# One transfer for the queries of a unit, a strided rounding to order them, and a reordered start, in an attention kernel with routed experts

## The chip, the cores and the metric

The kernel runs on one core of a Trainium2 chip. The metric is device time in microseconds (us), from the first to the last work of one execution; the time of a kernel is the median of its runs. The profile is one further execution, recorded by the hardware profiler.

## What is computed

Sliding-window attention with a linear distance bias, then a mixture of experts on its output. The reference, cut to what matters:

```python
# q, k, v: (8 batches, 8 heads, 576 positions, 64)
scores = scale * np.matmul(q, k.transpose(0, 1, 3, 2))
rel = pos[:, None] - pos[None, :]
mask = (rel >= 0) & (rel < 128)
scores = np.where(mask, scores + slopes[:, None, None] * -np.abs(rel), -1e9)
attn = softmax(scores)
x = np.matmul(attn, v).transpose(0, 2, 1, 3).reshape(4608, 512)

y_dense = np.maximum(x @ w1_dense, 0.0) @ w2_dense
expert_idx = np.argmax(x @ w_gate, axis=1)          # 8 experts
for e in range(8):                                   # the token's own expert only
    mask = expert_idx == e
    y_moe[mask] = gate_w[mask, None] * (np.maximum(x[mask] @ w1[e], 0.0) @ w2[e])
return y_dense + y_moe
```

## The kernel before

**Tiling.** Attention is cut into 16 units, `u` from 0 to 15: a batch and four of its eight heads. Each unit has three steps, `pr` 0, 1 and 2, over its five blocks of 128 keys (two, two and one). So there are 48 steps, numbered `n`, in one loop that issues work for several steps at once: scores of step `n`, the attend matmuls of step `n-1`, the normalization of step `n-2`, the transposes of the result (`flip`) of step `n-3`. Each batch, that is, each pair of units, also has a gate (which expert each token goes to), a dense layer in six items spread over the following steps, a scatter of its rows by expert to `xs_dram` and of its dense results to `ys_dram`. After the loop 43 blocks of 128 rows go through the experts (`block`).

**How queries and keys come in.** `load_k` (L125) brings the keys of a unit, 128 partitions by 1152 numbers (18 positions of 64), in one transfer in which each partition's 4608 bytes are one run in memory. `load_q` (L134) brings the queries in five transfers, one for each block of 128 positions, in which a partition gets 4 positions (1024 bytes; 2 positions, 512 bytes, in the last). On VectorE, `turn` (L159, instruction L162) transposes 32 by 32 pieces of either; its results are `ks` and `qs`. `round_qk` (L165) then rounds to the matmul's type on ScalarE: for keys L172 writes with a stride of 18 numbers, which puts the positions in their natural order (`kT`); for queries L169 copies straight through (`qT`), so that the queries within a block stay in another order. The bias mask, built from the iotas of L200 to L217, and the table of token numbers `tok_c` (L294 to L313) follow that order.

**Buffers.** There is one `kraw`, one `qraw`, one `qs` and one `qT` buffer; `kT` has two and the values `vf` three. A load of the next queries can thus start only when `turn` has read the last.

**What sets the order.** PE (TensorE), ACT (ScalarE) and DVE (VectorE) run in the order in which the code is written (`manual_schedule`, L1004). SP, the queue that issues most loads, runs in written order within the loop of 48 steps (L1021 to L1024); ahead of it and behind it, and on POOL (GpSimd), a scheduler orders. In step `pr` 0 of unit `u` stand `turn(u+1, "k")` and `load_k(u+2)`, in step 1 the rounding of the keys, `turn(u+1, "q")` and `load_q(u+2)`, in step 2 `load_v(u+2)`, the rounding of the queries and `prep_v(u+1)` (L182, which splits the values; result `vl`). On DVE L447 (`plo`) makes the low part of the probabilities `p` that ACT has exponentiated (L428), and L496 and L497 normalize (`recip`, `xf`).

**The start.** The queries of unit 0 are issued by ACT (three transfers) and SP (two). L376 is a one-column copy on POOL from the last queries into the values' buffer, which holds one load of the values back until the queries have come. `more_constants` (L279) sets up tables for the gate on DVE, between the transposes of unit 0's keys and queries. `mask_rest` (L275) makes the mask of heads 4 to 7 on ACT.

Of the kernel before, what the change touches and what calls it, by code (L numbers as in the profile page):

```python
# [23 lines left out]
def kernel(  # L24
# [99 lines left out]

    def load_k(u):  # L125
        b, hq = divmod(u, HQ)
        t = ld.tile([P, R, 2, 32], F32, name="kraw", tag="kraw")
        nc.sync.dma_start(
            out=t.rearrange("p r c d -> p (r c d)"),
            in_=k[b, 4 * hq : 4 * hq + 4].rearrange("h (p r) d -> (h p) (r d)", r=R),  # L130
        )
        raw[("k", u)] = t

    def load_q(u, eng):  # L134
        b, hq = divmod(u, HQ)
        hs = slice(4 * hq, 4 * hq + 4)
        t = ld.tile([P, R, 2, 32], F32, name="qraw", tag="qraw", bufs=1)
        for i in range(NT):
            n = 4 if i < NT - 1 else 2
            (eng[i] if isinstance(eng, tuple) else eng).dma_start(  # L140
                out=t[:, 4 * i : 4 * i + n, :, :].rearrange("p r c d -> p (r c d)"),
                in_=q[b, hs, i * P : i * P + 32 * n, :].rearrange(
                    "h (p r) d -> h p (r d)", r=n
                ),
            )
        raw[("q", u)] = t
# [18 lines left out]
    def round_qk(u, nm):  # L165
        s = tmp.pop((nm, u))
        if nm == "q":
            d = qtp.tile([P, 2, S], F32R, name="qT", tag="qT", bufs=1)
            nc.scalar.copy(out=d, in_=s)  # L169
        else:  # L170
            d = kTs[u % 2]
            nc.scalar.copy(  # L172
                out=d[:, :, 0:S].rearrange("p c (x r) -> p c r x", r=R),
                in_=s.rearrange("p c (r x) -> p c r x", r=R),
            )
        qkT[(nm, u)] = d

    def prep_v(u):
# [7 lines left out]

    load_k(0)
    load_q(0, (nc.scalar, nc.sync, nc.scalar, nc.sync, nc.scalar))


# [9 lines left out]
    nc.gpsimd.iota(  # L200
        d_i[:, 0:PW], pattern=[[P, 2], [1, 4], [4, 32]], base=0, channel_multiplier=-1
    )
    nc.gpsimd.iota(
        d_i[:, PW : PW + P], pattern=[[1, 4], [4, 32]], base=0, channel_multiplier=-1
    )
    nc.gpsimd.iota(
        d_i[:, PW + P : PW + P + TAIL],
        pattern=[[1, 2], [2, 32]],
        base=P,
        channel_multiplier=-1,  # L210
    )
    nc.gpsimd.iota(
        d_i[:, PW + P + TAIL : 2 * PW],
        pattern=[[1, 2], [2, 32]],
        base=0,
        channel_multiplier=-1,
    )  # L217
# [61 lines left out]
    def more_constants():  # L279
# [5 lines left out]
        for h in range(2):  # L285
# [8 lines left out]
        nc.vector.tensor_single_scalar(  # L294
            out=m_div, in_=pidx_i, scalar=5, op=ALU.logical_shift_right
        )
        nc.vector.tensor_single_scalar(
            out=m_mod, in_=pidx_i, scalar=31, op=ALU.bitwise_and
        )
        nc.vector.tensor_copy(out=m_divf, in_=m_div)  # L300
        nc.vector.tensor_copy(out=m_modf, in_=m_mod)
        for i in range(NT):
            nc.vector.scalar_tensor_tensor(
                out=tok_c[:, i : i + 1],
                in0=m_modf,
                scalar=4.0 if i < NT - 1 else 2.0,
                in1=m_divf,
                op0=ALU.mult,
                op1=ALU.add,
            )  # L310
            nc.vector.tensor_scalar_add(
                out=tok_c[:, i : i + 1], in0=tok_c[:, i : i + 1], scalar1=float(i * P)
            )  # L313
# [15 lines left out]
    m_div = consts.tile([P, 1], I32, name="m_div")  # L329
    m_mod = consts.tile([P, 1], I32, name="m_mod")  # L330
# [821 lines left out]
```

## Time and profile before

| | |
|---|---|
| time, median of 3 runs | 415.88 us (413.17 to 416.45) |
| the profiled execution's own time | 411.29 us |
| its span, first to last instruction | 409.6 us |
| PE busy | 339.0 us (83%) |
| DVE busy | 269.8 us (66%) |
| ACT busy | 261.6 us (64%) |
| POOL busy | 192.9 us (47%) |
| granted TensorE clock, mean | 0.953 of 2.4 GHz |

How to read the rows of the trace: an engine runs its instructions in order, each for the time shown; behind a row, in brackets, stands how long its engine sat idle before it and what released it. PE is TensorE's matmuls, PEld its weight loads. SPq and ACTq rows are the issuing of transfers, not the transfers. A span is not the sum of busy times: the five engines overlap, and what counts is who waits for whom.

### The profile page before, as it was taken

Reading aid. Unit: us, or ns where it says so; the run is one execution under the profiler, and the core shown is the slowest. Engines: PE = TensorE matmul, PEld = TensorE weight load, DVE = VectorE, ACT = ScalarE, POOL = GpSimd, SP = SyncE. Lnnn points to the kernel's source line nnn. Section 1 sums busy time; section 2 is a strip of 40 time slices with the busy share of each in tenths; the row PEclk is TensorE's granted clock in tenths of the full one; section 3 lists DMA queues with packets and bytes.
Section 4 is the critical chain, followed back from the end, with each engine's and each line's share of the span. In section 5 each row is a group of like instructions: output and inputs, shape, how many; then the busy total and the mean of one; then the engine's idle time right before and its main releaser. Section 6 shows DMA issues by size and latency. Waiting matters only on the chain.

```text
span 409.6 us, 12253 instructions
## 1 busy us (share of the span) xinstructions
PE 339.0 (83%) x4659; PEld 215.2 (53%) x4659; DVE 269.8 (66%) x525; ACT 261.6 (64%) x431; POOL 192.9 (47%) x245
## 2 busy tenths in 40 slices
PE   3458887979869998968997996978799799999990
PEld 0245666646555665645664764654455455555540
DVE  6668889787867986957897889752346344444440
ACT  6448847857856986984797786644356445555550
POOL 4012331654765447564566576353457434434431
PEclk9999959989978999997999998999999999999996
DMA  4565678859798779788696965429959999888730
GB/s 146 144 159 142 148 172 193 195 173 238 165 235 180 202 204 218 212 188 225 197 226 195 235 179 116 99 70 338 310 172 323 303 311 324 244 264 234 250 117 1
DMA packets 84986, 82.40 MB, mean 201 GB/s; under 512 B 43583, under 2 KB 71615, under 8 KB 84928
## 3 DMA queue, kind: packets, MB, share of 16 engines
q1 hardware_dynamic: 66852, 48.17, 41.2%
q0 software_dynamic: 17680, 33.12, 31.3%
q8 instruction: 38, 0.62, 0.6%
q10 hardware_dynamic: 396, 0.33, 0.3%
q14 instruction: 20, 0.16, 0.1%
HBM read 64.20 MB, written 28.66 MB: 227 GB/s over the span
## 4 chain that ended last, share of the span: by engine, by line
PE 30%; DMA 19%; DVE 18%; issue 13%; POOL 9%; SPq 6%; ACT 2%; POOLq 1%; ACTq 0%; DVEq 0%
DMA qraw<-in_q_dram 16%; POOL out_dram L973 6%; DVE plo L447 6%; PE yp L704 6%; PE ax L481 6%; SPq L140 5%; DVE qs L162 4%; PE hpm L937 3%; PE y L964 3%; PE hp L689 3%; DVE xf L497 2%; PE lg L566 2%; DMA xr<-xs_dram 2%; DMA xs_dram<-xrow,slot 2%; PE sq L417 1%
## 5 line engine op out<-in xcount | busy, mean ns | idle before, releaser
L481 PE MATMUL ax<-vf,p 128*128 128x65 bf16 (+1 forms) x576 | 66.6, 205 | 28.8 <-DVE xf L497 26.4
L447 DVE TENSOR_TENSOR plo<-p 128x1024 bf16<-128x1024 f32 (+1 forms) x96 | 85.2, 928 | 8.0 <-ACT p L428 7.9
L481 PEld LDWEIGHTS <-p 128*128 128x128 bf16 (+1 forms) x1152 | 62.9, 107 | 41.3 <-DVE xf L497 34.9
L428 ACT ACTIVATE p<-sq 128x1024 f32<-128x1024 f32 (+1 forms) x96 | 69.8, 784 | 4.8 <-PE sq L417 4.6
L973 POOL DMA_INDIRECT out_dram<-yo,xr x43 | 42.4, 986 | 64.5 <-DVE yo L972 54.1
L503 POOL CAST xrow<-xf 128x512 bf16<-128x512 f32 (+1 forms) x48 | 33.2, 700 | 71.5 <-DVE xf L497 66.7
L481 PE MATMUL ax<-vf,plo 128*128 128x65 bf16 (+1 forms) x576 | 66.1, 202 | 0.5 <-DVE plo L447 0.5
L481 PE MATMUL ax<-vl,p 128*128 128x64 bf16 (+1 forms) x576 | 66.2, 201 | 0.0
L481 PEld LDWEIGHTS <-plo 128*128 128x128 bf16 (+1 forms) x576 | 58.7, 106 | 0.7 <-DVE plo L447 0.7
L713 POOL DMA_INDIRECT ys_dram<-yt,slot x40 | 45.7, 1142 | 26.7 <-ACT yt L712 17.9
L643 POOL DMA_INDIRECT xs_dram<-xrow,slot x40 | 46.2, 1154 | 14.6 <-issue 10.2
L922 DVE COPY xTm<-xps 128x512 bf16<-128x512 bf16 x43 | 18.3, 424 | 50.1 <-PE xps L916 46.9
L696 ACT ACTIVATE hTd<-hp 128x256 bf16<-128x256 f32 (+1 forms) x64 | 26.4, 419 | 35.5 <-PE hp L689 34.6
L937 PE MATMUL hpm<-w_all,xTm 128*128 x172 | 44.0, 377 | 5.1 <-DVE yo L972 2.1
L704 PE MATMUL yp<-w_all,hTd 128*128 128x512 bf16 (+1 forms) x160 | 40.6, 381 | 6.7 <-DVE ltsb L559 5.0
L964 PE MATMUL y<-w_all,hTm 128*128 x172 | 44.1, 379 | 0.8 <-ACT hTm L956 0.8
L945 ACT ACTIVATE hr<-hpm,xr 128x512 bf16<-128x512 f32 x43 | 29.6, 687 | 22.5 <-PE hpm L937 19.3
L972 DVE TENSOR_TENSOR yo<-y,yr 128x512 f32<-128x512 f32 x43 | 29.7, 691 | 20.7 <-PE y L964 20.1
L689 PE MATMUL hp<-xTb,w_all 128*128 128x256 bf16 (+1 forms) x256 | 42.4, 296 | 0.6 <-ACT xTb L531 0.3
L956 ACT COPY hTm<-hps 128x512 bf16<-128x512 bf16 x43 | 25.2, 585 | 23.2 <-PE hps L952 23.2
L531 ACT COPY xT<-tp 128x512 f32<-128x512 f32 (+1 forms) x48 | 23.9, 498 | 23.3 <-PE tp L524 23.2
L417 PE MATMUL sq<-qT,kT 32*128 32x256 f32 (+2 forms) x640 | 32.0, 310 | 7.0 <-ACT qT L169 7.0
(146 smaller groups left out, 559.7 us busy)
## 6 DMA issues: line engine op xcount, KB each, us to landing
yr<-ys_dram SPq DMA_DIRECT2D x43, 256.0 KB
kraw<-in_k_dram SPq DMA_DIRECT2D x16, 576.0 KB
vf<-in_v_dram SPq DMA_DIRECT2D x64, 128.0 KB
w_all<-in_moe_w_dram POOLq DMA_DIRECT2D x16, 512.0 KB
qraw<-in_q_dram SPq DMA_DIRECT2D x62, 128.0 KB
xr<-xs_dram SPq DMA_DIRECT2D x43, 130.0 KB
ys_dram<-fill_x SPq DMA_DIRECT2D x8, 256.0 KB
xs_dram<-fill_x SPq DMA_DIRECT2D x8, 130.0 KB
```

The source lines that it names most:

```text
L417: nc.tensor.matmul(out=sq[g // 2][:, g % 2, i * wid : i * wid + nq], lhsT=kT[32 * g : 32 * g + 32, c, kj * P : kj * P + P], rhs=qT[32 * g ...
L428: nc.scalar.activation(out=p32[:, :, 0:tot], in_=sq[i][:, :, 0:tot], func=ACT.Exp, scale=SCALE,)
L447: nc.vector.tensor_tensor(out=plo[:, :, 0:tot], in0=p32[:, :, 0:tot], in1=phi[:, :, 0:tot], op=ALU.subtract,)
L481: nc.tensor.matmul(out=ax[:rows, i, o0 : o0 + w], lhsT=lhs, rhs=rhs, start=(n == 1), stop=(n == 3 * len(kl)),)
L503: nc.gpsimd.tensor_copy(out=xrow[:rows, qis[0] : qis[0] + nt, hq * 256 : hq * 256 + 256], in_=xf[:rows, 0:nt],)
L643: ins = nc.gpsimd.indirect_dma_start(out=xs_dram[:, :], out_offset=bass.IndirectOffsetOnAxis(ap=slot[:rows, t : t + 1], axis=0), in_=xrow. ...
L689: nc.tensor.matmul(out=hp[:, 0:HF], lhsT=w_all[:, E, 0, kc, c * P : c * P + P], rhs=xTb[:, kc, c0:c1], start=(kc == 0), stop=(kc == 3),)
L704: nc.tensor.matmul(out=yp[:rows, :], lhsT=hT[:, c, t0 * P : t0 * P + rows], rhs=w_all[:, E, 1, c, :], start=(c == 0), stop=(c == 3),)
L713: ins = nc.gpsimd.indirect_dma_start(out=ys_dram[:, :], out_offset=bass.IndirectOffsetOnAxis(ap=slots[b][:rows, t : t + 1], axis=0), in_=y ...
L937: nc.tensor.matmul(out=hp, lhsT=xT[:, kc, :], rhs=w_all[:, bass.DynSlice(er, 1), 0, kc, :], start=(kc == 0), stop=(kc == 3),)
L964: nc.tensor.matmul(out=y, lhsT=hT[:, c, :], rhs=w_all[:, bass.DynSlice(er, 1), 1, c, :], start=(c == 0), stop=(c == 3),)
L973: ins = nc.gpsimd.indirect_dma_start(out=out[:, :], out_offset=bass.IndirectOffsetOnAxis(ap=xr.bitcast(I32)[:, TC : TC + 1], axis=0), in_= ...
```

## The change

Queries are loaded as keys are, one transfer for each unit, with 18 consecutive positions in a partition. `round_qk` writes queries with the same stride of 18 as keys, so that `qT` is in natural order; the iotas of the mask and `tok_c` become plain, and ten small DVE instructions that made `tok_c` go. For unit 0 alone the rounding of the queries is on DVE, while ACT rounds the keys. SP runs in written order from the first load on. The copy L376 goes, unit 1's queries are issued by ACT, `load_v(1)` stands ahead of the loop, and `more_constants` moves from the start to behind the scores of step 1.

```diff
+    def load_qk(u, nm, eng):
+        b, hq = divmod(u, HQ)
+        t = ld.tile([P, R, 2, 32], F32, name=f"{nm}raw", tag=f"{nm}raw")
+        eng.dma_start(
+            out=t.rearrange("p r c d -> p (r c d)"),
+            in_={"q": q, "k": k}[nm][b, 4 * hq : 4 * hq + 4].rearrange(
+                "h (p r) d -> (h p) (r d)", r=R
+            ),
+        )
+        raw[(nm, u)] = t
...
     def load_q(u, eng):
-        b, hq = divmod(u, HQ)
-        hs = slice(4 * hq, 4 * hq + 4)
-        t = ld.tile([P, R, 2, 32], F32, name="qraw", tag="qraw", bufs=1)
-        for i in range(NT):
-            n = 4 if i < NT - 1 else 2
-            (eng[i] if isinstance(eng, tuple) else eng).dma_start(
-                out=t[:, 4 * i : 4 * i + n, :, :].rearrange("p r c d -> p (r c d)"),
-                in_=q[b, hs, i * P : i * P + 32 * n, :].rearrange(
-                    "h (p r) d -> h p (r d)", r=n
-                ),
-            )
-        raw[("q", u)] = t
+        load_qk(u, "q", eng)
...
-    def round_qk(u, nm):
+    def round_qk(u, nm, copy=nc.scalar.copy):
         s = tmp.pop((nm, u))
         if nm == "q":
             d = qtp.tile([P, 2, S], F32R, name="qT", tag="qT", bufs=1)
-            nc.scalar.copy(out=d, in_=s)
         else:
             d = kTs[u % 2]
-            nc.scalar.copy(
-                out=d[:, :, 0:S].rearrange("p c (x r) -> p c r x", r=R),
-                in_=s.rearrange("p c (r x) -> p c r x", r=R),
-            )
+        copy(
+            out=d[:, :, 0:S].rearrange("p c (x r) -> p c r x", r=R),
+            in_=s.rearrange("p c (r x) -> p c r x", r=R),
+        )
...
+    ctx.enter_context(tc.manual_schedule(engines={ENG.SP}))
     load_k(0)
-    load_q(0, (nc.scalar, nc.sync, nc.scalar, nc.sync, nc.scalar))
+    load_q(0, nc.scalar)
...
         for i in range(NT):
-            nc.vector.scalar_tensor_tensor(
-                out=tok_c[:, i : i + 1],
-                in0=m_modf,
-                scalar=4.0 if i < NT - 1 else 2.0,
-                in1=m_divf,
-                op0=ALU.mult,
-                op1=ALU.add,
-            )
             nc.vector.tensor_scalar_add(
-                out=tok_c[:, i : i + 1], in0=tok_c[:, i : i + 1], scalar1=float(i * P)
+                out=tok_c[:, i : i + 1], in0=pidx_f, scalar1=float(i * P)
             )
...
-    nc.gpsimd.tensor_copy(out=vfs[0][:, 0, 0, 0:1], in_=raw[("q", 0)][:, R - 1, 1, 31:32])
     load_v(0)
     wg_load()
...
         round_qk(0, "k")
-        more_constants()
+        turn(0, "q")
+        round_qk(0, "q", nc.vector.tensor_copy)
         mask_rest()
-        turn(0, "q")
-        round_qk(0, "q")
         load_k(1)
-        load_q(1, nc.sync)
+        load_q(1, nc.scalar)
+        load_v(1)
...
-        loads = ExitStack()
-        loads.enter_context(tc.manual_schedule(engines={ENG.SP}))
         while jm < NB:
-            if n == NS:
-                loads.close()
...
-            if n == 0:
-                load_v(1)
+            if n == 1:
+                more_constants()
```

The order on DVE at the start, before: `ks_190` and `qs_231` are unit 0's transposed keys and queries, `ks_287` and `qs_376` unit 1's, and the 29 rows from `ut_b_150` to `fill_x_164` are `more_constants`, most of them left out here.

```order
L162 STREAM_TRANSPOSE ks_190<-kraw_103 128x18x2x32
L281 CAST ut_b_150<-hTd_115 128x128
L294 TENSOR_SCALAR m_div_153<-pidx_i_120 128x1
L324 CAST fill_x_164<-oob_f_165 128x1
L162 STREAM_TRANSPOSE qs_231<-qraw_105 128x18x2x32
L182 TENSOR_TENSOR vl_285<-vf0_131 128x1280
L162 STREAM_TRANSPOSE ks_287<-kraw_235 128x18x2x32
L447 TENSOR_TENSOR plo_281<-p32_279 128x1024
L162 STREAM_TRANSPOSE qs_376<-qraw_237 128x18x2x32
L447 TENSOR_TENSOR plo_337<-p32_335 128x1024
L496 RECIPROCAL recip_419<-ax_338 128x8
```

The same engine and place in the changed kernel, where `ks_183` and `qs_190` are unit 0's, `ks_249` and `qs_333` unit 1's:

```order
L156 STREAM_TRANSPOSE ks_183<-kraw_105 128x18x2x32
L156 STREAM_TRANSPOSE qs_190<-qraw_107 128x18x2x32
L165 CAST qT_192<-qs_190 128x2x18x32
L175 TENSOR_TENSOR vl_247<-vf0_129 128x1280
L156 STREAM_TRANSPOSE ks_249<-kraw_198 128x18x2x32
L410 TENSOR_TENSOR plo_243<-p32_241 128x1024
L156 STREAM_TRANSPOSE qs_333<-qraw_200 128x18x2x32
L410 TENSOR_TENSOR plo_294<-p32_292 128x1024
L266 CAST ut_b_148<-hTd_113 128x128
L293 CAST fill_x_158<-oob_f_159 128x1
L459 RECIPROCAL recip_393<-ax_295 128x8
```

The constants now stand behind the second step's `plo` and ahead of the first normalization, and the rounding of unit 0's queries is in the row that was ACT's.

On SP, the queue of loads, the start before: `kraw_103` and `qraw_105` are of unit 0, `kraw_235` and `qraw_237` of unit 1.

```order
L128 DMA kraw_103<-in_k_dram 128x1152
L140 DMA qraw_105<-in_q_dram 128x1x256 x2
L154 DMA vf0_131<-in_v_dram 128x4x64 x3
L154 DMA vf0_131<-in_v_dram 64x4x64
L365 DMA wg_pad_167<-in_moe_w_gate_dram 128x4x8
L154 DMA vf0_131<-in_v_dram 128x4x64
L128 DMA kraw_235<-in_k_dram 128x1152
L140 DMA qraw_237<-in_q_dram 128x1x256 x4
L140 DMA qraw_237<-in_q_dram 128x1x128
L128 DMA kraw_289<-in_k_dram 128x1152
```

And in the changed kernel, where unit 0's and unit 1's queries are ACT's and `qraw_335` is unit 2's:

```order
L128 DMA kraw_105<-in_k_dram 128x1152
L148 DMA vf0_129<-in_v_dram 128x4x64 x4
L148 DMA vf0_129<-in_v_dram 64x4x64
L329 DMA wg_pad_161<-in_moe_w_gate_dram 128x4x8
L128 DMA kraw_198<-in_k_dram 128x1152
L148 DMA vf1_132<-in_v_dram 128x4x64 x4
L148 DMA vf1_132<-in_v_dram 64x4x64
L128 DMA kraw_251<-in_k_dram 128x1152
L128 DMA qraw_335<-in_q_dram 128x1152
```

Five rows of queries for each unit have become one, and all values of unit 0 follow its keys directly. From unit 2 on the order of keys, queries and values is that of before.

On ACT the start before (`kT0_140` is unit 0's rounded keys, `qT_233` its queries; the mask rows behind `kT0_140` are heads 4 to 7):

```order
L172 CAST kT0_140<-ks_190 128x2x18x32
L271 ACTIVATE mask_111<-yt_114 128x512
L271 ACTIVATE mask_111<-ax_185 128x512 x2
L271 ACTIVATE mask_111<-hp_186 128x512
L169 CAST qT_233<-qs_231 128x1152
L428 ACTIVATE p32_279<-sq0_245 128x1024
```

and after:

```order
L165 CAST kT0_138<-ks_183 128x2x18x32
L256 ACTIVATE mask_109<-yt_112 128x512
L256 ACTIVATE mask_109<-ax_178 128x512 x2
L256 ACTIVATE mask_109<-hp_179 128x512
L128 DMA qraw_200<-in_q_dram 128x1152
L391 ACTIVATE p32_241<-sq0_207 128x1024
```

Unit 0's rounding of queries is gone from ACT, and the issue of unit 1's queries stands ahead of its first exponentials. Apart from these places, the rows of PE, DVE, ACT and POOL keep their order, POOL's without L376; on SP the part behind the loop keeps its order too.

## Rows read from the trace of the kernel before

**Rows 1.** The page: chain of work that ended last, by line.
```profile
DMA qraw<-in_q_dram 16%; POOL out_dram L973 6%; DVE plo L447 6%; PE yp L704 6%; PE ax L481 6%; SPq L140 5%; DVE qs L162 4%; PE hpm L937 3%; PE y L964 3%; PE hp L689 3%; DVE xf L497 2%; PE lg L566 2%; DMA xr<-xs_dram 2%; DMA xs_dram<-xrow,slot 2%; PE sq L417 1%
```
**Rows 2.** DVE's waits, 0 to 260 us: total, times, longest.
```profile
DVE qs L162 <- DMA qraw<-in_q_dram: 11.7, 6, 4.1
```
**Rows 3.** Windows: stretch, length, PE, PEld, DVE, ACT, POOL busy; PEclk, DMA share, GB/s.
```profile
13.50:15.00 1.50, 0.67 (x12) 0.67 (x16) 0.81 (x1) 0.78 (x1) 0.00 (x0) 1.00 0.95 300
16.50:18.50 2.00, 1.52 (x20) 0.58 (x23) 1.76 (x2) 1.03 (x2) 0.00 (x0) 1.00 0.27 94
```
**Rows 4.** Timeline, units 0 and 1: start, us, engine, line, operation, [idle before].
```profile
12.26 0.46 SPq L128 DMA_DIRECT2D kraw<-in_k_dram  x1
13.12 3.27 SPq L140 DMA_DIRECT2D qraw<-in_q_dram  x5
...
15.60 1.94 ACT L428 ACTIVATE p<-sq 128x1024 f32<-128x1024 f32 x2 [1.31 <-PE sq L417]
...
16.73 1.38 DVE L162 STREAM_TRANSPOSE ks<-kraw 128x1152 f32<-128x1152 f32 x1 [1.05 <-DMA kraw<-in_k_dram]
...
19.38 1.94 ACT L428 ACTIVATE p<-sq 128x1024 f32<-128x1024 f32 x2 [1.84 <-PE sq L417]
...
23.41 1.38 DVE L162 STREAM_TRANSPOSE qs<-qraw 128x1152 f32<-128x1152 f32 x1 [3.06 <-issue]
...
26.95 0.20 DVE L496 RECIPROCAL recip<-ax 128x8 f32<-128x8 f32 x1
```
**Rows 5.** Timeline of the start, DVE and ACT.
```profile
4.69 1.38 DVE L162 STREAM_TRANSPOSE ks<-kraw 128x1152 f32<-128x1152 f32 x1 [0.77 <-DMA kraw<-in_k_dram]
...
5.99 0.18 DVE L281 CAST ut_b<-hTd 128x128 bf16<-128x128 f32 x1
...
6.80 0.15 DVE L294 TENSOR_SCALAR m_div<-pidx_i 128x1 int32<-128x1 int32 x1
...
8.53 0.17 DVE L314 CAST em<-hTd 128x40 f32<-128x40 int32 x1
...
9.84 0.15 DVE L324 CAST fill_x<-oob_f 128x1 int32<-128x1 f32 x1
10.08 0.63 ACT L271 ACTIVATE mask<-hp 128x512 bf16<-128x512 f32 x1
```
**Rows 6.** ACT's groups by line: busy, mean ns of one | idle before, releaser.
```profile
L172 ACT CAST kT<-ks 128x1152 fp32r<-128x1152 f32 x16 | 37.5, 2345 | 0.0
...
L712 ACT COPY yt<-yp 128x512 f32<-128x512 f32 (+1 forms) x40 | 23.5, 587 | 20.5 <-PE yp L704 20.5
...
L169 ACT CAST qT<-qs 128x1152 fp32r<-128x1152 f32 x16 | 18.4, 1147 | 3.5 <-DVE qs L162 3.5
```
**Rows 7.** Timeline of DVE, one batch without a wait for queries.
```profile
132.94 1.38 DVE L162 STREAM_TRANSPOSE qs<-qraw 128x1152 f32<-128x1152 f32 x1
...
143.36 2.36 DVE L447 TENSOR_TENSOR plo<-p 128x1024 bf16<-128x1024 f32 x2 [0.40 <-ACT p L428]
...
156.03 0.69 DVE L497 TENSOR_TENSOR xf<-ax,recip 128x512 f32<-128x512 f32 x1 [2.28 <-POOL w_all L732]
...
163.41 1.38 DVE L162 STREAM_TRANSPOSE qs<-qraw 128x1152 f32<-128x1152 f32 x1
```
**Rows 8.** Timelines of POOL, ACT and PE in the same batch.
```profile
151.39 0.24 POOL L636 TENSOR_SCALAR xrow<-tok_c 128x5 int32<-128x5 f32 x1 [4.14 <-DMA xs_dram<-xrow,slot]
...
155.57 1.96 ACT L428 ACTIVATE p<-sq 128x1024 f32<-128x1024 f32 x2
...
159.01 2.02 PE L704 MATMUL yp<-w_all,hTd 128*128 128x512 bf16 x8
```
**Rows 9.** Timeline of DVE: a wait in unit 3, and where two batches begin.
```profile
50.98 1.38 DVE L162 STREAM_TRANSPOSE qs<-qraw 128x1152 f32<-128x1152 f32 x1 [1.44 <-DMA qraw<-in_q_dram]
...
65.92 1.38 DVE L162 STREAM_TRANSPOSE qs<-qraw 128x1152 f32<-128x1152 f32 x1
...
228.56 1.38 DVE L162 STREAM_TRANSPOSE qs<-qraw 128x1152 f32<-128x1152 f32 x1
```

More of the change, by code (lines that the diff above doesn't have):

```diff
@@ L123 @@
     vparts = {}
-    def load_k(u):
-        b, hq = divmod(u, HQ)
[L127 to L130, printed above, removed]
-        )
-        raw[("k", u)] = t
-    def load_q(u, eng):
-        b, hq = divmod(u, HQ)
-        hs = slice(4 * hq, 4 * hq + 4)
-        t = ld.tile([P, R, 2, 32], F32, name="qraw", tag="qraw", bufs=1)
-        for i in range(NT):
-            n = 4 if i < NT - 1 else 2
-            (eng[i] if isinstance(eng, tuple) else eng).dma_start(
-                out=t[:, 4 * i : 4 * i + n, :, :].rearrange("p r c d -> p (r c d)"),
-                in_=q[b, hs, i * P : i * P + 32 * n, :].rearrange(
-                    "h (p r) d -> h p (r d)", r=n
-                ),
-            )
-        raw[("q", u)] = t
+    def load_qk(u, nm, eng):
[8 more added lines that the diff above has]
+        raw[(nm, u)] = t
+    def load_k(u):
+        load_qk(u, "k", nc.sync)
+    def load_q(u, eng):
+        load_qk(u, "q", eng)
     def load_v(u):
@@ L199 @@
     sh = sh.rearrange("p c x -> p (c x)").bitcast(F32)
[L200 to L217, printed above, removed]
+    for c0, w, base in (
+        (0, PW, 0),
+        (PW, P, 0),
+        (PW + P, TAIL, P),
+        (PW + P + TAIL, TAIL, 0),
+    ):
+        nc.gpsimd.iota(
+            d_i[:, c0 : c0 + w], pattern=[[1, w]], base=base, channel_multiplier=-1
+        )
     pidx_i = consts.tile([P, 1], I32, name="pidx_i")
@@ L293, in more_constants @@
             )
[L294 to L301, printed above, removed]
-        for i in range(NT):
-            nc.vector.scalar_tensor_tensor(
-                out=tok_c[:, i : i + 1],
-                in0=m_modf,
-                scalar=4.0 if i < NT - 1 else 2.0,
-                in1=m_divf,
-                op0=ALU.mult,
-                op1=ALU.add,
-            )
+        for i in range(NT):
             nc.vector.tensor_scalar_add(
-                out=tok_c[:, i : i + 1], in0=tok_c[:, i : i + 1], scalar1=float(i * P)
+                out=tok_c[:, i : i + 1], in0=pidx_f, scalar1=float(i * P)
             )
@@ L328 @@
     sel = consts.tile([P, 2, E], F32, name="sel")
-    m_div = consts.tile([P, 1], I32, name="m_div")
-    m_mod = consts.tile([P, 1], I32, name="m_mod")
-    m_divf = consts.tile([P, 1], F32, name="m_divf")
-    m_modf = consts.tile([P, 1], F32, name="m_modf")
     tok_c = consts.tile([P, NT], F32, name="tok_c")
```

## The prediction

> **What bounds the kernel now.** I read the chain of work that ended last first, since it says which line's lateness the end hangs on. One line stands far ahead: the transfer of queries holds 16% of the span, and its issue by SP another 5% [rows 1]. A share of the chain is not what can be won: it says where the chain ran, and a second chain may run close beside it. So next come the waits of DVE. It sat idle for the queries six times, 11.7 us in all, once for 4.1 us [rows 2]; the wait of 3.06 us in unit 1 is put down to "issue", but the queries are what was late there as well [rows 4].
>
> Why are they late? Keys and queries of a unit have the same 576 KB. The windows show a stretch in which keys alone come in: 0.95 of the 16 DMA engines' time, 300 GB/s. In one in which queries alone come in it is 0.27 and 94 GB/s [rows 3], so about four engines carry them. In unit 1 the keys are issued at 12.26 and used at 16.73, by a DVE that waited for them: 4.5 us. The queries are issued from 13.12, in five pieces that take SP 3.27 us, and used at 23.41: 10.3 us [rows 4]. There is one buffer, so the next load starts only behind the transpose, and transpose, issue and landing form a loop.
>
> Last I read the timeline of a batch (two units) without such a wait, since this is what is left when the waits go. It runs from 132.94 to 163.41, 30.5 us. DVE waited there 0.40 us for ACT's exponentials at 143.36 and 2.28 us for POOL at 156.03 [rows 7], and POOL had itself waited 4.14 us for the scatter to land [rows 8]. The five batches from 65.92 to 228.56 take 162.6 us [rows 9], 32.5 on average.
>
> **The change part by part.** *One transfer instead of five.* It has the form of the keys, so I give it the keys' 4.5 us from issue to use, against 10.3. Below that no row goes; above, I bound it by 7 us, for a transfer that meets the values and the experts' weights. A batch of 30.5 us holds two such loops, 15 us each on average, so even 7 us is covered, and all waits for queries go. SP also issues 7 loads a unit in place of 11. What is late next is the price of the following part and POOL's chain.
>
> *The strided rounding on ACT.* The keys' rounding shows its price: 2.345 us against 1.147, 1.2 us more for each of units 1 to 15 [rows 6]. In units 1 to 3, ahead of the first dense layer, ACT has least to do, and I count nothing; 3.6 (3 x 1.2) if that is wrong. In a batch it has two places. In the first unit ACT runs rounding, two copies, then the exponentials that DVE waited 0.40 us for at 143.36 [rows 7] (one of five such rows, one in each batch, all with 0.40): DVE moves by the whole 1.2. It takes this to 156.03, where it waited 2.28 for POOL anyway, so there it is absorbed. In the second unit the rounding starts 1.2 later and lasts 1.2 longer, and the exponentials of 155.57 [rows 8] go to 157.97. DVE has a transpose of keys to do meanwhile; PE hands out dense results, and its third tile needs the copy of the first to have left PSUM, a copy that stands behind both exponentials on ACT: 157.97 + 1.96 + 0.59 = 160.5, then 1.0 of matmuls (half of 2.02), 161.5 to 161.9 with the hand-overs, against 161.03 before [rows 6, 8]. The gate's matmuls follow, and they end the batch. So a batch becomes 30.5 + 0.7 = 31.2. Bounds: 30.5 if it is hidden, 32.9 (30.5 + 2 x 1.2) if POOL's cover is gone. I take 31.2, since the cover is in the rows.
>
> Five batches: 5 x 31.2 = 156.0 against 162.6, a gain of **6.6**. In the last batch one of the shorter waits goes and a rounding of 1.2 us comes; I count them as even: **0**. In units 1 to 3 the wait of 1.44 at 50.98 goes [rows 9]: **1.4**.
>
> *The start.* The queries of unit 0 are issued by ACT at the moment of the keys. Alone they would be there 4.5 us later, at 5.3. The keys were used at 4.69 [rows 5]; if queries and values, 1152 KB, share what follows at 300 GB/s, queries may be there as late as 3.9 us behind that, at 8.6 (estimates from rows 3 to 5). I take 7.0, between them. Transpose 1.4 to 8.4; rounding on DVE has no row: by DVE's `plo`, 2.36 for two of 1024 numbers [rows 7], 1.3 for 1152 numbers, by ACT's slowdown for the stride twice that. I take 1.3, since ACT covers the other: it ends its masks at 10.71 [rows 5] and issues queries for some 0.5 us, so that its exponentials cannot start ahead of 11.2. Scores need 1.3 behind the rounding [rows 4]: 11.0. So exponentials start at 11.2 in place of 15.60, and the second pair 3.8 later as before [rows 4], at 15.0. Unit 1's keys wait for the transpose that ends at 6.07, are issued about 6.5 and used at 11; its queries are issued about 11.2 and used at 15.7 in place of 23.41. Transpose and `plo` (1.4 + 2.3) end at 19.4.
>
> Now the moved constants: from 5.99 to 9.99 they stood in DVE's wait for unit 0's queries, at no cost. Fourteen instructions, 6.80 to 8.53, become five, say 0.5: 4.0 - 1.7 + 0.5 = 2.8 us [rows 5]. At their new place nothing hides them: DVE's normalization is queued behind, PE's next attend matmuls wait for that. 19.4 + 2.8 = 22.2, normalization at 22.3 in place of 26.95: a gain of **4.5**, between 2.5 (queries at 17.7) and 6.
>
> On the issue by ACT, rows first: with three of the five pieces issued by ACT at once with the keys, the keys were still used at 4.69, 0.77 after DVE was free [rows 5]. The Trainium skill (DMA: Bandwidth & Descriptors, "Queues, rings and completion order") says that each DMA engine takes turns between the queues that have work for it. By that rule a full-width transfer on ACT's queue takes half of each engine from the keys, which are needed first; the keys would land some 1.2 us later, the start would gain 3.3 in place of 4.5 and the sum be 404.4. The sum here goes by the row.
>
> *The rest.* The plain iotas and the removed copy on POOL lie beside the loads, which end later: nothing, and they are too small to move the range without that cover. SP's written order changes no row behind the loop. The natural order of tokens changes which rows stand together in a block, not how many or how large.
>
> **Sum.** 4.5 + 1.4 + 6.6 + 0 = 12.5 us. The expert blocks behind attention start that much earlier and take what they took. 411.29 - 12.5 = 398.8 for the profiled execution, whose span is 409.6. The median of the runs shown, 415.88, is 1.1% above it; scaled, the prediction is **403 us**.
>
> **The rivals.** *The rounding costs nothing.* If ACT's longer work falls into gaps everywhere, batches are at 30.5 or, with a scatter that lands sooner, 29.5: 10.2 to 15.2 from the batches, 16 to 21 in all, 395 to 400. For it: ACT is 64% busy. Against it: the five waits of 0.40.
>
> *Something else holds the batches.* If the scatter's landing, or values in a fuller queue, hold a batch at 32.5, only the start and unit 3 gain: 5.9, that is 410. The same comes out if one transfer is no faster in company, which is the case that the change does not do what it says. For it: POOL's wait of 4.14. Against it: the batch of rows 7 ran in 30.5 with that wait in it.
>
> *Slower: the rounding is paid twice in each batch.* If the waits for queries only covered POOL's chain, and the chain through ACT's rounding ran in series with it, a batch would be 32.5 + 2.4 = 34.9; six of them cost 14.4, less 5.9 from the start: 8.5 more, 424. It decides from a batch of 33.7 on (32.5 + 5.9/5). Against it: DVE's waits of 0.40 and 2.28 lie one behind the other, the second open to the first.
>
> **How the numbers follow.** Forecast 0.50 (its own range 399 to 408), free rounding 0.27, something else 0.16 (407 to 415), slower 0.07. The range 394 to 411 leaves out the slower case, the upper half of "something else" and a little below. One per cent is about what a measurement of this kernel tells from no change: faster by more (below 411.7) has 0.50, 0.27 and 0.06 of the third case, 0.83; within it 0.10; slower 0.07.
>
> **What would show it.** Right: no wait of DVE for queries behind unit 0; one transfer's stretch near 300 GB/s; the rounding of queries at about 2.35 us; DVE's wait for exponentials in the first unit of a batch grown from 0.40 to about 1.6, and that for POOL shrunk; batches of 31.2; the first normalization near 22.3. Wrong: waits for queries that stay; batches near 30 or above 33; constants that cost more than 2.8; or expert blocks that take longer than before.

## The result and the profile after

The changed kernel takes 397.34 us (396.34 to 400.16, 4 runs) against 415.06 of the kernel before beside it: a ratio to the kernel before of 0.959 (95% interval 0.953 to 0.964), 17.7 us less. The prediction was 403, range 394 to 411, faster; the time lies in the range, below the likeliest case's own 399 to 408. Its profiled execution took 400.16, with a span of 398.4; the profiled one of before took 411.29.

The chain of work that ended last, by line:

```profile
DVE plo L410 11%; PE ax L444 10%; PE yp L667 9%; POOL out_dram L936 6%; ACT qT L165 6%; PE hpm L900 4%; DVE xf L460 4%; DVE qs L156 3%; PE y L927 3%; PE hp L652 3%; PE sq L380 2%; PE lg L529 2%; ACT p L391 2%; DMA qraw<-in_q_dram 2%; DMA xr<-xs_dram 2%
```

The transfer of queries, 16% in [rows 1], holds 2%, and its issue by SP has left the list. New on it is ACT's rounding of queries, 6%.

DVE's waits from 0 to 260 us (total, times, longest), the counterpart of [rows 2]:

```profile
DVE plo L410 <- ACT p L391: 19.1, 13, 1.8
...
DVE ks L156 <- DMA kraw<-in_k_dram: 2.7, 1, 2.7
...
DVE xf L460 <- POOL w_all L695: 1.7, 2, 0.9
...
DVE qs L156 <- DMA qraw<-in_q_dram: 1.0, 1, 1.0
```

11.7 us of waits for queries have become one of 1.0, in unit 1. The waits for ACT's exponentials have grown; in the kernel before the same stretch had

```profile
DVE plo L447 <- ACT p L428: 7.5, 10, 1.5
```

Of the issues on the page, queries now land as keys do:

```profile
kraw<-in_k_dram SPq DMA_DIRECT2D x16, 576.0 KB, 5.2
...
qraw<-in_q_dram SPq DMA_DIRECT2D x14, 576.0 KB, 4.6
```

The start on DVE, beside [rows 4, 5]:

```profile
6.60 1.38 DVE L156 STREAM_TRANSPOSE ks<-kraw 128x1152 f32<-128x1152 f32 x1 [2.72 <-DMA kraw<-in_k_dram]
7.90 1.34 DVE L156 STREAM_TRANSPOSE qs<-qraw 128x1152 f32<-128x1152 f32 x1
9.27 1.25 DVE L165 CAST qT<-qs 128x1152 fp32r<-128x1152 f32 x1
...
16.55 1.38 DVE L156 STREAM_TRANSPOSE qs<-qraw 128x1152 f32<-128x1152 f32 x1 [1.00 <-DMA qraw<-in_q_dram]
...
20.09 0.22 DVE L266 CAST ut_b<-hTd 128x128 bf16<-128x128 f32 x1
...
22.57 0.15 DVE L293 CAST fill_x<-oob_f 128x1 int32<-128x1 f32 x1
22.64 0.20 DVE L459 RECIPROCAL recip<-ax 128x8 f32<-128x8 f32 x1
```

The first normalization is at 22.64 in place of 26.95, though the keys came 1.9 us later than in [rows 5]. One batch on DVE, beside [rows 7]:

```profile
121.51 1.37 DVE L156 STREAM_TRANSPOSE qs<-qraw 128x1152 f32<-128x1152 f32 x1
...
133.06 2.36 DVE L410 TENSOR_TENSOR plo<-p 128x1024 bf16<-128x1024 f32 x2 [1.54 <-ACT p L391]
...
143.47 0.69 DVE L460 TENSOR_TENSOR xf<-ax,recip 128x512 f32<-128x512 f32 x1 [0.86 <-POOL w_all L695]
...
147.50 2.36 DVE L410 TENSOR_TENSOR plo<-p 128x1024 bf16<-128x1024 f32 x2 [1.66 <-ACT p L391]
...
152.52 1.37 DVE L156 STREAM_TRANSPOSE qs<-qraw 128x1152 f32<-128x1152 f32 x1
```

It takes 31.0 us. The wait for exponentials has grown from 0.40 to 1.54 in the first unit, one of 1.66 is new in the second, and the wait for POOL has shrunk from 2.28 to 0.86. All five batches take 31.0 us, where those of before take 30.3 to 34.8.

Last the stages, as windows: up to unit 4, the five batches to unit 14, the rest of attention, the expert blocks (length, busy time of PE, PEld, DVE, ACT, POOL, granted clock as a share of 2.4 GHz, DMA share, GB/s). First the kernel before, then the changed one:

```profile
0.00:65.92 65.92, 40.95 (x709) 29.04 (x709) 49.16 (x92) 41.30 (x55) 16.67 (x47) 0.92 0.63 154
65.92:228.56 162.64, 142.01 (x2476) 95.72 (x2480) 128.13 (x215) 123.07 (x209) 92.61 (x110) 0.95 0.82 203
228.56:273.30 44.74, 38.05 (x681) 26.67 (x678) 37.02 (x92) 31.22 (x57) 23.97 (x26) 0.96 0.53 136
273.30:409.60 136.30, 118.03 (x802) 63.76 (x802) 55.51 (x126) 65.97 (x112) 59.67 (x63) 0.97 0.75 243
```

```profile
0.00:59.50 59.50, 40.53 (x709) 28.23 (x709) 48.76 (x85) 43.27 (x54) 16.54 (x46) 0.89 0.73 179
59.50:214.60 155.10, 135.90 (x2464) 92.37 (x2478) 126.39 (x217) 134.04 (x209) 94.03 (x110) 1.00 0.88 215
214.60:261.20 46.60, 39.19 (x682) 26.38 (x678) 36.43 (x94) 33.56 (x57) 25.28 (x26) 0.93 0.46 114
261.20:398.40 137.20, 118.21 (x787) 64.46 (x800) 55.70 (x126) 66.02 (x112) 59.70 (x63) 0.96 0.74 241
```

So 6.4 us were won up to unit 4 and 7.5 in the five batches; 1.9 were lost in the rest of attention and 0.9 in the blocks, both at a lower granted clock: 11.2 us of span. In the batches the clock went from 0.95 to 1.00, and PE does its matmuls there in 135.9 us in place of 142.0. In the kernel before, the two batches in which DVE's transposes of queries waited for nothing (30.5 and 30.3 us) ran at 1.00, and the three in which they waited (33.0, 34.0 and 34.8 us) at 0.95, 0.90 and 0.90. How much of the longer three is the wait itself and how much the clock is not separated; the batch of [rows 7] and those of the changed kernel can be compared, both at 1.00.

### The profile page after: what moved, and what is told of

Read it like the earlier page. It is cut to its first block, busy times and chain, and to the rows that moved or that the text cites. A ratio compares the mean times of both kernels' runs of the same rounds, so it can differ in the third digit from the quotient of the medians.

```text
span 398.4 us, 12103 instructions
## 1 busy us (share of the span) xinstructions
PE 333.8 (84%) x4631; PEld 211.4 (53%) x4659; DVE 267.3 (67%) x517; ACT 276.9 (70%) x430; POOL 195.6 (49%) x244
## 4 chain that ended last, share of the span: by engine, by line
PE 36%; DVE 25%; issue 13%; ACT 11%; POOL 6%; DMA 5%; SPq 1%; POOLq 1%; DVEq 0%; ACTq 0%
DVE plo L410 11%; PE ax L444 10%; PE yp L667 9%; POOL out_dram L936 6%; ACT qT L165 6%; PE hpm L900 4%; DVE xf L460 4%; DVE qs L156 3%; PE y L927 3%; PE hp L652 3%; PE sq L380 2%; PE lg L529 2%; ACT p L391 2%; DMA qraw<-in_q_dram 2%; DMA xr<-xs_dram 2%
## 5 line engine op out<-in xcount | busy, mean ns | idle before, releaser
L444 PE MATMUL ax<-vf,p 128*128 128x65 bf16 (+1 forms) x576 | 63.7, 201 | 15.0 <-DVE xf L460 13.7
L444 PEld LDWEIGHTS <-p 128*128 128x128 bf16 (+1 forms) x1152 | 60.1, 104 | 27.9 <-DVE xf L460 21.2
L444 PE MATMUL ax<-vl,p 128*128 128x64 bf16 (+1 forms) x576 | 63.2, 198 | 0.0
L444 PE MATMUL ax<-vf,plo 128*128 128x65 bf16 (+1 forms) x576 | 63.0, 198 | 0.0
L676 POOL DMA_INDIRECT ys_dram<-yt,slot x40 | 47.5, 1186 | 30.4 <-ACT yt L675 22.6
L444 PEld LDWEIGHTS <-plo 128*128 128x128 bf16 (+1 forms) x576 | 57.3, 104 | 0.0
L606 POOL DMA_INDIRECT xs_dram<-xrow,slot x40 | 45.1, 1127 | 14.4 <-issue 10.1
L667 PE MATMUL yp<-w_all,hTd 128*128 128x512 bf16 (+1 forms) x147 | 41.9, 397 | 3.7 <-DVE ltsb L522 1.5
L652 PE MATMUL hp<-xTb,w_all 128*128 128x256 bf16 (+1 forms) x256 | 40.7, 289 | 0.6 <-ACT xTb L494 0.3
L165 ACT CAST kT<-ks 128x1152 fp32r<-128x1152 f32 x16 | 37.5, 2344 | 1.4 <-DVE ks L156 1.4
```

What stands on the lines that cost most here:

```text
L165: copy(out=d[:, :, 0:S].rearrange("p c (x r) -> p c r x", r=R), in_=s.rearrange("p c (r x) -> p c r x", r=R),)
L444: nc.tensor.matmul(out=ax[:rows, i, o0 : o0 + w], lhsT=lhs, rhs=rhs, start=(n == 1), stop=(n == 3 * len(kl)),)
L606: ins = nc.gpsimd.indirect_dma_start(out=xs_dram[:, :], out_offset=bass.IndirectOffsetOnAxis(ap=slot[:rows, t : t + 1], axis=0), in_=xrow. ...
L652: nc.tensor.matmul(out=hp[:, 0:HF], lhsT=w_all[:, E, 0, kc, c * P : c * P + P], rhs=xTb[:, kc, c0:c1], start=(kc == 0), stop=(kc == 3),)
L667: nc.tensor.matmul(out=yp[:rows, :], lhsT=hT[:, c, t0 * P : t0 * P + rows], rhs=w_all[:, E, 1, c, :], start=(c == 0), stop=(c == 3),)
L676: ins = nc.gpsimd.indirect_dma_start(out=ys_dram[:, :], out_offset=bass.IndirectOffsetOnAxis(ap=slots[b][:rows, t : t + 1], axis=0), in_=y ...
```

## The experiments

Theory: the one transfer removes the waits for queries; what is left of the change is a strided rounding that costs ACT 1.2 us a unit and some 0.7 us a batch, and a start that brings 4.5 us. Rivals: the stride is free; the stride is paid in both units; the reordered start brings nothing by itself. The runs fell on three chips, on which the kernel before took 441.05 (e1 to e4), 415.42 (e7, e1b, e2b, e8) and 414.02 us (e3b, e5, e9, e10); times are compared only within such a group, or by the ratio to the kernel before.

### First group, on the slower chip

**e1_before_start**: the changed kernel with the start of before.

```diff
-    ctx.enter_context(tc.manual_schedule(engines={ENG.SP}))
+    nc.gpsimd.tensor_copy(out=vfs[0][:, 0, 0, 0:1], in_=raw[("q", 0)][:, R - 1, 1, 31:32])
...
-        turn(0, "q")
-        round_qk(0, "q", nc.vector.tensor_copy)
+        more_constants()
         mask_rest()
+        turn(0, "q")
+        round_qk(0, "q")
```

> The changed kernel with the start of before: one transfer of queries per unit and the strided rounding on ACT stay, but the copy that holds back a load of values, the constants ahead of unit 0's queries, unit 1's queries on SP and the rounding of unit 0's queries on ACT are back. If the queries' transfer carries most of the gain (17.7 us between the medians) and the start its 4.5 us, this takes 397.3 + 4.5, about 402 us, with the first normalization at 25 to 27 us of the span. If the gain that the sum did not hold (17.7 against 12.5) came from the start, it takes 406 us or more. If the start's gain is lost again later, it takes 397 to 399 us.

436.36 us (433.76 to 442.8), ratio 0.990 (0.986 to 0.995). A miss: on this chip one transfer with the start of before gains 1%.

**e2_start_alone**: the kernel before with the start of the changed one (the same lines, the other way round; the five transfers of unit 0, and those of unit 1, all on ACT's queue).

> The kernel before with the start of the changed one alone: queries still in five transfers and copied straight through. If transpose, issue and landing of the five transfers form the loop that binds the early units, the first normalization comes some 3 us earlier, but waits for queries in units 2 to 5 grow by part of it: a gain of 1 to 3.5 us on 415, 411.5 to 414. If the start's gain passes whole to the end, 4.5 us: 410.5. If the start carries the larger part of the change, 405 or less.

453.5 us, ratio 1.032 (1.021 to 1.044): slower, where a gain was expected in every case.

**e3_plain_rounding**: the changed kernel with the rounding of queries without its stride.

```diff
-        copy(
-            out=d[:, :, 0:S].rearrange("p c (x r) -> p c r x", r=R),
+        if nm == "q":
+            copy(out=d, in_=s)
+        else:
```

> The changed kernel with the queries' rounding written straight through, 1.15 us in place of 2.35 on ACT; the queries of a unit then stand in another order than the mask and the scatter assume, so part of the computation (which query meets which bias) is changed, and the work is the same. If the stride costs 0.7 us a batch, as in the prediction, 397.3 - 4 = 393 us. If it is hidden everywhere, 397. If it is paid twice in each batch in series, 2.4 us by six, 383. DVE's waits for exponentials, 19.1 us in the changed kernel, should fall to about 8 in the first and last case.

435.68 us (431.33 to 438.16), ratio 0.989 (0.980 to 0.998): no different from e1_before_start, so that none of the three cases can be told on this chip.

**e4_strided_transpose**: the stride moved from ACT to DVE's transposes, both roundings on ACT in a row.

```diff
-        nc.vector.transpose(out=s.rearrange("p c (r x) -> p r c x", r=R), in_=t)
+        nc.vector.transpose(out=s.rearrange("p c (x r) -> p r c x", r=R), in_=t)
```

> The changed kernel with the stride moved: DVE's transposes of keys and queries write with the stride of 18, in natural order, and ACT rounds both straight through, 1.15 us in place of 2.35 for each. If DVE writes with a stride at the speed it writes without (in the changed kernel its strided rounding of unit 0's queries took 1.25 us for 1152 numbers), ACT is relieved by 2.4 us a unit and the time falls below that of the plain rounding of queries alone, to 389 to 394. If the stride slows DVE's transpose as it slows ACT's copy, from 1.37 to 2.6 us twice a unit, DVE, which is nearly full in the first unit of each batch, pays up to 2.4 us a unit: 400 to 430.

451.8 us (446.79 to 455.36), all four runs above all thirteen of the kernel before (436.39 to 446.75). DVE's groups by line (busy, mean ns of one):

```profile
L156 DVE STREAM_TRANSPOSE ks<-kraw 128x1152 f32<-128x1152 f32 x16 | 37.3, 2331 | 2.8 <-DMA kraw<-in_k_dram 2.8
L156 DVE STREAM_TRANSPOSE qs<-qraw 128x1152 f32<-128x1152 f32 x16 | 37.2, 2324 | 0.0
```

A transpose that writes with the stride takes 2.33 us in place of 1.37 to 1.38 [rows 7]. The stride costs 0.95 us there against 1.20 in ACT's copy [rows 6], and it is now paid on DVE: the second theory, in direction.

On this chip the five batches took 34.7 to 36.1 us each on average in these four kernels. Of e1_before_start, where DVE waits for no queries either, the first took 32.9 us at a granted clock of 1.00 and the others 35.8 to 37.2 at 0.91 to 0.95. DVE waited 38.6 us for exponentials in the five, where the same program on the next chip waited 16.5; PE was busy 29.3 to 30.5 us in each of the last four, where it was 27.2 to 27.4 in the changed kernel's of the other chips. Whether the waits brought the lower clock or the clock the waits, and why the first batch is already longer, is open. Since this hides what the change moves in the batches, the same kernels were run again.

### Second group

**e7_changed_again**: the changed kernel itself.

> The changed kernel once more, beside the kernel before, for a common base with the runs of this call: the first comparison gave a ratio of 0.959, and the first experiments ran on a chip on which the kernel before took 441 us in place of 415. Theory 1 (the gain comes from the waits for queries and the start, which are the same on any chip): ratio 0.955 to 0.97, on a chip of 415 as on one of 441. Theory 2 (on the slower chip batches are held by other work, from unit 4 on, so that only the first units gain): on a chip of 441 us a ratio of 0.985 to 0.995; on one of 415 us 0.96. In both: keys of unit 0 used at 6.6, first normalization at 22.6.

397.73 us (395.44 to 399.71), as in the first comparison (397.34), so that this group can be read with it. The kernel before took 415.42 beside it, but spread widely: two of its seven runs took 408.5 and 410.6, the other five 415.2 to 418.8. So the runs of this group are read against the changed kernel where they can be. With e1_before_start's 0.990 on the slower chip, the two cases of theory 2 came as it gave them. Its profiled execution, windows as above:

```profile
0.00:57.40 57.40, 37.42 (x709) 26.34 (x709) 48.60 (x85) 43.25 (x54) 16.54 (x46) 1.00 0.76 185
57.40:212.40 155.00, 136.42 (x2472) 92.40 (x2476) 126.25 (x216) 133.97 (x209) 93.96 (x110) 1.00 0.91 216
212.40:257.60 45.20, 38.13 (x685) 26.05 (x682) 36.45 (x93) 33.64 (x58) 25.01 (x27) 0.96 0.47 114
257.60:393.70 136.10, 118.31 (x802) 63.62 (x802) 55.69 (x126) 65.91 (x112) 59.73 (x63) 0.98 0.75 243
```

The batches are the same to 0.1 us. The first stretch is 2.1 us shorter, at a clock of 1.00 in place of 0.89 (PE 37.4 us in place of 40.5 for the same 709 matmuls), the rest of attention 1.4 at 0.96 in place of 0.93, the blocks 1.1 at 0.98 in place of 0.96. The 4.7 us between the two spans, 393.7 and 398.4, lie almost wholly where the clock differs.

**e1b_before_start**: as e1_before_start.

> One transfer and the strided rounding with the start of the kernel before, a second time, now beside the changed kernel. Theory A (the reordered start brings some 4 us of its own): 4 us above the changed kernel. Theory B (the start gains by the one transfer alone; what the reordering brings in unit 1, 3 us, the constants take back in unit 1 to 2, since in the first run with this start unit 4 began at 58.1 against 59.5): equal to the changed kernel within 1.5 us, and first normalization at 23.3.

397.21 us (395.51 to 397.69), equal to the changed kernel. Its start on DVE:

```profile
6.68 1.38 DVE L156 STREAM_TRANSPOSE ks<-kraw 128x1152 f32<-128x1152 f32 x1 [2.80 <-DMA kraw<-in_k_dram]
...
10.49 1.37 DVE L156 STREAM_TRANSPOSE qs<-qraw 128x1152 f32<-128x1152 f32 x1
...
19.20 1.37 DVE L156 STREAM_TRANSPOSE qs<-qraw 128x1152 f32<-128x1152 f32 x1
...
22.98 0.20 DVE L459 RECIPROCAL recip<-ax 128x8 f32<-128x8 f32 x1
```

With the start of before, but one transfer, the first normalization is at 22.98 against 22.64. Theory B holds: the reordering wins 2.65 us up to unit 1's queries (16.55 against 19.20), and the constants, in the open at their new place, take back 2.6.

**e2b_start_alone**: as e2_start_alone.

> The start of the changed kernel with the five transfers and the plain rounding of the kernel before, a second time. Theory A (the reordered start is worth some 4 us by itself): 4 us below the kernel before. Theory B (the reordered start needs the one transfer: five narrow transfers on ACT's queue land at 12.9 and 26.4, as in the first run of this kernel, against 11.7 and 23.4): 5 to 12 us above the kernel before; unit 4 begins at 72 against 65.9.

416.43 us (414.66 to 418.42). The gain of theory A did not come. Whether the loss of theory B did is open: the runs lie 4 to 10 us above the two shortest of the kernel before, and level with the other five. In the start theory B holds, and unit 4 began at 72.0, as it said:

```profile
13.14 1.38 DVE L162 STREAM_TRANSPOSE qs<-qraw 128x1152 f32<-128x1152 f32 x1 [6.55 <-DMA qraw<-in_q_dram]
14.56 0.76 DVE L169 CAST qT<-qs 128x1152 fp32r<-128x1152 f32 x1
...
26.50 1.38 DVE L162 STREAM_TRANSPOSE qs<-qraw 128x1152 f32<-128x1152 f32 x1 [4.76 <-DMA qraw<-in_q_dram]
...
33.98 0.20 DVE L496 RECIPROCAL recip<-ax 128x8 f32<-128x8 f32 x1
```

Five pieces from ACT's queue alone come later than from two, 13.14 against 11.72, and the first normalization is 7.0 us behind that of [rows 4]. Part of the 7.0 are the constants, which now stand ahead of it.

**e8_dve_rounding**: the changed kernel with all roundings of queries on DVE.

```diff
-                        round_qk(u + 1, "q")
+                        round_qk(u + 1, "q", nc.vector.tensor_copy)
```

> The changed kernel with the rounding of queries on DVE in every unit, not in unit 0 alone. DVE took 1.25 us for it in unit 0, ACT 2.35 in the others, and DVE waits 13 times, 19.1 us in all, for exponentials that stand behind it on ACT. Theory 1 (the rounding on ACT's queue holds the batches): DVE's waits for exponentials shrink to some 8 us, each batch gives back 0.5 to 1.5 net of the 2.5 that DVE works more, in all 3 to 8 us below the changed kernel. Theory 2 (the batch is a ring through all engines and DVE's own row of work is as long): DVE's 15 x 1.25 = 19 us take the place of the waits, equal within 2 us. Theory 3 (DVE becomes the bound): 5 us or more above.

388.56 us (388.02 to 389.57), 9.2 below the changed kernel: a little more than theory 1 gave. Its batches take 29.6 us. The waits of DVE, 0 to 260 us:

```profile
DVE plo L410 <- ACT p L391: 1.1, 1, 1.1
```

and one batch as a window:

```profile
89.10:118.70 29.60, 27.36 (x506) 18.71 (x502) 27.63 (x47) 22.96 (x42) 20.71 (x23) 1.00 0.92 229
```

The waits for exponentials are gone but for one, and DVE, busy 27.6 of 29.6 us, is now the fullest engine, with PE at 27.4 next.

### Third group

**e3b_plain_rounding**: as e3_plain_rounding.

> The changed kernel with the rounding of queries without its stride: ACT reads and writes 1152 numbers in a row (the queries then stand in a different order, so the attention is that of other rows; the amount of work is the same). ACT's 2.35 us become 1.15 as before the change. Theory 1 (the prediction's step: the stride costs 0.7 us a batch, in the second unit alone): a batch of 30.3 in place of 31.0, 4 us below the changed kernel. Theory 2 (DVE waits in both units of a batch for exponentials that stand behind the rounding, 1.55 and 1.65 us, so the 1.2 us count twice): a batch of 28.6 to 29, 11 to 14 us below the changed kernel, also below the kernel that rounds queries on DVE (9 below).

383.67 us (382.99 to 387.41), ratio 0.929 (0.920 to 0.938). Against the 0.959 of the changed kernel that is 12 us, and 14 between the medians: theory 2. A batch, on DVE:

```profile
145.21 1.37 DVE L156 STREAM_TRANSPOSE qs<-qraw 128x1152 f32<-128x1152 f32 x1
...
155.62 2.36 DVE L413 TENSOR_TENSOR plo<-p 128x1024 bf16<-128x1024 f32 x2 [0.40 <-ACT p L394]
...
165.88 0.69 DVE L463 TENSOR_TENSOR xf<-ax,recip 128x512 f32<-128x512 f32 x1 [0.72 <-POOL xrow L469]
...
168.90 2.36 DVE L413 TENSOR_TENSOR plo<-p 128x1024 bf16<-128x1024 f32 x2 [0.65 <-ACT p L394]
...
173.87 1.37 DVE L156 STREAM_TRANSPOSE qs<-qraw 128x1152 f32<-128x1152 f32 x1
```

It takes 28.7 us, 2.3 less than with the stride and 1.8 less than the batch of before in [rows 7]. Both waits for exponentials are 1.0 to 1.1 shorter than in the changed kernel. On PE the waits of the scores for the rounding (from 60 to 229 us) are gone altogether; the row is that of the changed kernel, e3b_plain_rounding has none:

```profile
PE sq L380 <- ACT qT L165: 12.2, 11, 1.1
```

**e5_first_queries_on_sp**: the queries of unit 0 from SP, behind the keys.

```diff
-    load_q(0, nc.scalar)
+    load_q(0, nc.sync)
```

> The changed kernel with the queries of unit 0 issued by SP, behind the keys, in place of ACT. Theory 1 (on two queues keys and queries of unit 0 come in side by side and the keys, needed first, land later): keys used at 4.7 to 5.2 in place of 6.6, queries at about the same 7.9 to 8.5, exponentials of unit 0 up to 1 us earlier or, since the masks stand ahead of them on ACT, at 11.2 to 12; the whole 0 to 1 us below the changed kernel. Theory 2 (the keys are late for another reason, the start of the first transfer or the values): keys at 6.6 still, no change.

394.95 us (393.09 to 397.72), ratio 0.952 (0.944 to 0.960). In the start:

```profile
5.06 1.38 DVE L156 STREAM_TRANSPOSE ks<-kraw 128x1152 f32<-128x1152 f32 x1 [1.18 <-DMA kraw<-in_k_dram]
6.66 1.38 DVE L156 STREAM_TRANSPOSE qs<-qraw 128x1152 f32<-128x1152 f32 x1 [0.22 <-DMA qraw<-in_q_dram]
...
21.62 0.20 DVE L459 RECIPROCAL recip<-ax 128x8 f32<-128x8 f32 x1
```

Theory 1: behind one another on one queue both are used sooner, the keys by 1.5 us, the queries by 1.2, and the first normalization comes 1.0 sooner. That this makes the kernel faster, its interval cannot tell from the changed kernel's.

**e9_constants_first**: e8_dve_rounding with the constants ahead of the first transpose.

```diff
         mask_consts()
+        more_constants()
         turn(0, "k")
...
-            if n == 1:
-                more_constants()
```

> The kernel that rounds all queries on DVE, with the constants for the gate ahead of the first transpose of keys, where DVE waits 2.6 to 2.8 us for the keys, in place of behind the scores of step 1, where they took 2.6 us in the open. If the constants are on the path there: keys used at 6.6 to 7.2, first normalization near 20.8 in place of 22.7 and 1 to 2.5 us below the kernel that rounds queries on DVE (ratio to the kernel before 0.930 to 0.934 in place of 0.935). If units 1 to 3 have room for them: no change.

387.96 us (386.28 to 389.36), ratio 0.935 (0.927 to 0.944); e8_dve_rounding took 388.56 (388.02 to 389.57) in the second group. The first normalization came at 20.65 in place of 21.64 there, but in the whole no difference is shown.

**e10_before_again**: the kernel before, for a second trace.

> The kernel before once more with a profile. Its profiled execution took 411.3, while the median of its other runs is 415 to 416; the changed kernel's took 400.2 and 395.4 against a median of 397. Theory 1 (the profiled execution of before was a quick one, and a usual one loses 4 us more to waits for queries): qs of unit 14 at 231 to 233 in place of 228.6, waits for queries above 11.7 us. Theory 2 (the usual one loses them behind the attention, to TensorE's clock): qs of unit 14 at 228 to 229, a lower granted clock behind it. Ratio to itself 1.00 in both.

413.11 us (409.54 to 420.19), ratio 0.997 (0.993 to 1.001). The profiled execution was the longest of these, 420.19, and so no more a usual one than the first. Unit 14 began at 230.3, and 188.1 us follow it in place of 181.0, at a clock of 0.95. Its waits for queries:

```profile
DVE qs L162 <- DMA qraw<-in_q_dram: 17.9, 7, 4.2
```

They were 11.7 in the first profile of the kernel before: they change from one execution to the next. Neither theory is settled by this trace.

The fastest kernels here that order the queries as the reference needs are e8_dve_rounding and e9_constants_first, not told apart: 388 to 389 us, some 9 below the changed kernel.

## Why the prediction was right

**Waits for queries.** Right but for one wait of 1.0 us in unit 1, where none was to be left behind unit 0. One transfer lands in 4.6 us (predicted 4.5 from issue to use).

**The batch.** 31.0 measured, 31.2 predicted, and by the chain that the prediction followed: in the second unit ACT's exponentials begin 24.9 us into the batch (146.45 - 121.51), 25.0 by its working (157.97 - 132.94):

```profile
146.45 1.02 ACT L391 ACTIVATE p<-sq 128x1024 f32<-128x1024 f32 x1
```

Yet two steps ahead of that number were wrong and cancelled, and that 31.2 came out is luck. *The stride costs 0.7 a batch* was mis-sized: e3b_plain_rounding shows 2.3, that is, both roundings in full. And *a batch without the stride is 30.5* was too long: it is 28.7. The clock does not explain this: in the batch of [rows 7], in those of e3b_plain_rounding and in those of the changed kernel it is 1.00. The step that failed in both is that the 2.28 us in which DVE waits for POOL [rows 7] were taken as given, a cover for the first unit's 1.2. That wait came with the five transfers and shrank with them, to 0.72 in e3b_plain_rounding. POOL's waits for the scatter to land, 60 to 229 us, first in the kernel before, then in e1b_before_start, which has its start but one transfer and the stride:

```profile
POOL xrow L636 <- DMA xs_dram<-xrow,slot: 18.3, 5, 5.0
```

```profile
POOL xrow L599 <- DMA xs_dram<-xrow,slot: 7.3, 5, 1.8
```

With five transfers it is 17.1 to 18.3 us (before, e2b_start_alone, e10_before_again), with one 7.3 to 11.4 (e1b_before_start, e3b_plain_rounding, the changed kernel, e8_dve_rounding, e7_changed_again), with the stride as without it. Nor does it hold the batches of the changed kernel any more: POOL waits there between 0 and 3.8 us for the scatter, and every batch takes 31.0. What of the one transfer brings the scatter in sooner is not shown: the narrow pieces themselves, the loads that SP issues beside them, which drop from 11 to 7 a unit, or the order of the tokens, which changed along with it. The rival "the rounding costs nothing" had named a scatter that lands sooner, as a gain; it came, and the stride took it. The rival "paid twice in each batch" was right in what the stride costs and wrong in what it is added to: 28.7 + 2.3, not 32.5 + 2.4.

**Units 1 to 3.** Right to count nothing for the stride there: unit 4 begins at 59.2 without it and at 57.4 and 59.5 with it.

**The start.** Right in size: first normalization at 22.64 (22.3 predicted, which is a gain of 4.65, where the sum carried 4.5), rounding on DVE 1.25 (1.3), constants from 20.09 to 22.6, 2.6 us (2.8; fourteen of their instructions became five, so that nine went, and not the ten that the description of the change names). Start and unit 3 together were to bring 5.9; unit 4 began 6.4 earlier, and 8.5 in e7_changed_again, at the full clock. Wrong in what it is owed to: e1b_before_start has the one transfer without the reordering and loses nothing that can be measured, and e2b_start_alone has the reordering without the one transfer and gains nothing.

**Keys beside queries.** Here the step that went by the row failed. The keys, at 4.69 with three narrow pieces beside them [rows 5], came at 6.60 with one wide transfer on ACT's queue, and at 5.06 when that transfer stood behind them on SP's. The Trainium skill (DMA: Bandwidth & Descriptors, "Queues, rings and completion order") says that the engines take turns between queues; the trace agrees, with 1.5 us between the last two where 1.2 had been worked out. The sum did not suffer, because queries and unit 1's keys came early enough: the exponentials began at 12.11 in place of the 11.2 predicted, and what stands behind them was 0.3 late in the end:

```profile
12.11 1.04 ACT L391 ACTIVATE p<-sq 128x1024 f32<-128x1024 f32 x1
```

**The last batch and the blocks.** Predicted 0; the profiled execution lost 2.8 there, e7_changed_again 0.3, with the clock.

**From profile to median.** The sum, 12.5, gives 398.8 for the profiled execution; the two of the changed kernel took 400.16 and 395.44, gains of 11.1 and 15.9 on the profiled 411.29. Multiplying by 1.011 was the step that made 403 out of it, and it failed: it carried the distance between the profiled run of before and its median over to a kernel whose runs all lie between 395.4 and 400.2. Of the 5.7 us by which the prediction lies above 397.34, 4.2 come from there. The rest, 1.5, is less than two executions differ by.

## What to carry to other kernels

A wait that seems to cover an added cost has a cause of its own: ask whether the change removes that cause too, before it is used as cover. What one operand's layout saves in the transfer comes back where it is written in another order, so price that on every engine that could do it: here moving the strided copy from the waited-for engine to another won a further 9 us, half of what the change had won. The ratio of the old kernel's median to its profile need not hold for the new kernel: here it did not, and where it comes from stayed open.

## What the runs showed of the hardware

- Writing 1152 numbers of 4 bytes per partition with a stride of 18 costs each operation something different: a copy on ACT takes 2.35 us in place of 1.15, a copy on DVE 1.25 in place of 0.76, DVE's transpose 2.33 in place of 1.37.
- In the kernels that load queries in five narrow pieces POOL waited 17.1 to 18.3 us for its scatters (60 to 229 us), in those with one transfer 7.3 to 11.4. That the narrow pieces themselves delay the scatter is not shown.
- With the waits for queries gone, the granted clock in the five batches was 1.00 in place of 0.95, and PE needed some 6 us less for the same matmuls, which the prediction's sum of waits does not contain. On the slower chip e1_before_start had no such waits either, and 0.94; so more than these waits goes with the clock.
- One program, e1_before_start and e1b_before_start, took 436 us on one chip and 397 on another. DVE and ACT were busy equally long within 1%; PE was busy 346.9 us at a mean clock of 0.94, against 334.0 at 0.97. The first 58 to 59 us, up to unit 4, were no slower.
